# A gated recurrence and a causal-convolution unit: 1024-token chunks, the gated input on GpSimd, pairs of tokens transposed as 32-bit words

## Chip, cores, metric

One core of one Trainium2 chip (trn2). The metric is the device time in microseconds of one execution; medians are over all executions of a run, ratios over its fast ones.

## The reference, cut

Inputs `x`, `r_gate`, `i_gate` are (4, 6336, 256) in fp32: 25,344 tokens of 256 channels.

```python
log_a = 8.0 * sigmoid(r_gate) * log(clip(sigmoid(a_param), 1e-6, 1 - 1e-6))
a_t = exp(log_a)
x_gated = sqrt(max(1 - a_t * a_t, 1e-6)) * sigmoid(i_gate) * x
for t in range(S):                      # the scan, fresh in each of the 4 sequences
    h = a_t[:, t] * h + x_gated[:, t]
    y[:, t] = h
gate = sigmoid(causal_conv(y, conv_w))  # 5 taps per channel
out = (gate * (y @ w_val)) @ w_out
```

## The kernel before

Tokens arrive on the partitions; the scan wants channels there, so gates and products are transposed on TensorE. All sigmoids are tanh with a factor of a half: the input gate is (1 + tanh)/2. Windows are 512 tokens.

```python
# loads: 128 partitions x 4 runs of 1 KB (one token each)
nc.sync.dma_start(dst, src[t0:t0 + nj * P, :].rearrange("(j p) d -> p j d", p=P))
# tanh of both gates (ScalarE), u = (tanh + 1) * x in one VectorE instruction
nc.scalar.activation(out=tri[...], in_=ri[...], func=ACT.Tanh, scale=0.5)
nc.vector.scalar_tensor_tensor(out=uring[...], in0=tri[:, 1, ...], scalar=1.0, in1=xt[...], op0=ALU.add, op1=ALU.mult)
# a = exp(...) (ScalarE, from the transposed gate), a*a (GpSimd), sqrt in batches (ScalarE)
nc.gpsimd.tensor_tensor(out=ering[...], in0=a, in1=a, op=ALU.mult)
# xg = transpose(u) * norm, then the scan: both inputs in SBUF
nc.vector.tensor_tensor(out=xg[...], in0=uT[...], in1=nh[...], op=ALU.mult)
nc.vector.tensor_tensor_scan(out=yb[...], data0=aring[...], data1=xg[...], initial=..., op0=ALU.mult, op1=ALU.add)
# ... cut: conv as 5 diagonal 128x128 matmuls a half, val, gv = (tanh + 1) * val, out, copies, store
```

Of the kernel before, what the change touches and what calls it, by code (L numbers as in the profile page):

```python
# [8 lines left out]
P = 128  # L9
WIN = 512  # L10
SUB = WIN // P
CONV_K = 5
C_SCALE = 8.0
NS = 11
NY = 7
NIN = 3
NTRI = 3
NOSB = 3
MIN_UNIT = [1, 2, 3, 4]
COST = dict(load=4.5, tanh=1.9, u2=1.3, srT=0.5, uT=0.5, exp=1.45, e=2.15, xg=0.66, scan=2.7, conv=2.4, tg=0.97,  # L20
            val=0.95, gv=1.16, out=0.47, osbD=0.64, osbA=0.62, sq=0.88, sq0=0.2, table=1.3, store=1.5,
            sem=0.15, dma=2.2)
FP32 = mybir.dt.float32
# [5 lines left out]
def make_plan(frac):  # L29




    nw = len(frac)
    nq = [max(1, round(2 * f)) for f in frac]
    qwin = [(g, i) for g in range(nw) for i in range(nq[g])]
    qlast = [sum(nq[:g + 1]) - 1 for g in range(nw)]
    done, nxt, free = {}, {}, {}
    order, units = [], []
    mode = "E"  # L40

    def at(op):
        return nxt.get(op, 0)

    while True:
        cands = []

        def cand(op, eng, dur, deps, prio, i, n=1):
            t = 0.0
            for d in deps:  # L50
                if d[1] < 0:
                    continue
                if d not in done:
                    return
                t = max(t, done[d] + COST["sem"])
            if eng == "ACT" and op != "osb" and (op == "sq") != (mode == "S"):
                dur = dur + COST["table"]
            cands.append((max(free.get(eng, 0.0), t), prio, op, eng, dur, i, n))

        def per_window(op, eng, prio, deps, limit=nw):  # L60
            g = at(op)
            if g < limit:
                cand(op, eng, COST[op] * frac[g], [(d, g + o) for d, o in deps], prio, g)

        nsq = at("sq")
        per_window("load", "DMA", 0, [("tanh", -NIN), ("u2", -NIN)])
        per_window("tanh", "ACT", 3, [("load", 0), ("srT", -NTRI), ("u2", -NTRI)])
        per_window("u2", "DVE", 0, [("tanh", 0), ("uT", -NS)])
        per_window("srT", "PE", 0, [("tanh", 0), ("exp", -2)])
        per_window("exp", "ACT", 1, [("srT", 0), ("scan", -NS), ("e", -NS)])  # L70
        per_window("e", "POOL", 0, [("exp", 0), ("xg", -NS)])
        per_window("uT", "PE", 1, [("u2", 0), ("xg", -1)], nsq)
        per_window("xg", "DVE", 3, [("uT", 0), ("sq", 0), ("scan", -1)], nsq)
        per_window("scan", "DVE", 2, [("xg", 0), ("val", -NY)], nsq)
        per_window("conv", "PE", 3, [("scan", 0), ("tg", -1)])
        per_window("tg", "ACT", 0, [("conv", 0), ("gv", -2)])
        per_window("val", "PE", 2, [("conv", 0), ("gv", -1)])
        g = at("gv")
        if g < nw:
            cand("gv", "DVE", COST["gv"] * frac[g],  # L80
                 [("tg", g), ("val", g), ("out", qlast[g - 2] if g >= 2 else -1)], 1, g)
        q = at("out")
        if q < len(qwin):
            cand("out", "PE", COST["out"], [("gv", qwin[q][0]), ("osb", q - 1)], 1, q)
        q = at("osb")
        if q < len(qwin):
            for e, eng in (("D", "DVE"), ("A", "ACT")):
                cand("osb", eng, COST["osb" + e], [("out", q), ("store", qwin[q][0] - NOSB)], 0.5, q)
        g = at("store")
        if g < nw:  # L90
            cand("store", "DMA", COST["store"] * frac[g], [("osb", qlast[g])], -1, g)

        n = at("e") - nsq
        if n and mode == "E":
            all_in = at("exp") == nw
            stuck = at("e") == at("exp") and (all_in or ("scan", at("exp") - NS) not in done
                                              and at("exp") >= NS)
            low = (nsq - at("scan")) * (COST["xg"] + COST["scan"]) <= 2 * COST["table"] + COST["sq"] * n
            enough = n >= min(MIN_UNIT[min(len(units), len(MIN_UNIT) - 1)], nw - nsq)
            if stuck or (low and enough):  # L100
                cand("sq", "ACT", COST["sq0"] + COST["sq"] * sum(frac[nsq:nsq + n]),
                     [("e", nsq + n - 1)], -1, nsq, n)
        if not cands:
            break
        t, prio, op, eng, dur, i, n = min(cands)
        free[eng] = t + dur
        order.append((t, op, i, eng, n))
        nxt[op] = i + n
        for k in range(i, i + n):
            done[(op, k)] = t + dur + (COST["dma"] if eng == "DMA" else 0.0)  # L110
        if op == "sq":
            units.append(n)
        if eng == "ACT" and op != "osb":
            mode = "S" if op == "sq" else "E"
    assert at("store") == nw
    order.sort(key=lambda o: o[0])
    return order, qwin
# [3 lines left out]
def kernel(  # L121
# [15 lines left out]
    T = B * S  # L137

# [4 lines left out]

    nwin = (T + WIN - 1) // WIN
    ntok = [min(WIN, T - g * WIN) for g in range(nwin)]

    segs = []
    for g in range(nwin):
        t0, t1 = g * WIN, g * WIN + ntok[g]
        cuts = [t0] + [c for c in range(S, T, S) if t0 < c < t1] + [t1]  # L150
        segs.append([(c0 - t0, c1 - t0, c0 % S == 0) for c0, c1 in zip(cuts[:-1], cuts[1:])])
    YW = WIN + 4 * max(len(s) for s in segs)

    plan, qwin = make_plan([n / WIN for n in ntok])

    const = ctx.enter_context(tc.tile_pool(name="const", bufs=1))
    inp = ctx.enter_context(tc.tile_pool(name="inp", bufs=3))
    live = {}

    def load(g):  # L160
        nj = ntok[g] // P
        t0 = g * WIN
        ri = inp.tile([P, 2, SUB, D], FP32, name="ri", tag="ri", bufs=NIN)
        xt = inp.tile([P, SUB, D], FP32, name="xt", tag="xt", bufs=NIN)
        for dst, src in ((ri[:, 0, 0:nj, :], rf), (ri[:, 1, 0:nj, :], if_), (xt[:, 0:nj, :], xf)):
            nc.sync.dma_start(dst, src[t0:t0 + nj * P, :].rearrange("(j p) d -> p j d", p=P))
        live["ri", g], live["xt", g] = ri, xt

    with tc.manual_schedule():
        ap2 = const.tile([H, P], FP32, name="ap2")  # L170
        nc.sync.dma_start(ap2[:], a_param.rearrange("(h p) -> h p", p=P))
        wrow = const.tile([CONV_K, D], FP32, name="wrow")
        nc.sync.dma_start(wrow[:], moe_conv_w[:, :])
        for g in range(NIN):
            load(g)
# [7 lines left out]
        wv = const.tile([P, H, D], BF16, name="wv")  # L183
        nc.gpsimd.dma_start(wv[:], moe_w_val.rearrange("(hk p) n -> p hk n", p=P))
        wo = const.tile([P, H, D], BF16, name="wo")
        nc.gpsimd.dma_start(wo[:], moe_w_out.rearrange("(hk p) n -> p hk n", p=P))
        khf = const.tile([P, H], FP32, name="khf")
        wcol = const.tile([P, H, CONV_K], FP32, name="wcol")
        with tc.tile_pool(name="ps_setup", bufs=1, space=bass.MemoryType.PSUM) as ps_setup:
            kps = ps_setup.tile([P, H], FP32, name="kps")  # L190
            nc.tensor.transpose(out=kps[:], in_=ap2[0:H, :], identity=ident_f[0:H, 0:H])
            kt = const.tile([P, H], FP32, name="kt")
            nc.scalar.activation(out=kt[:], in_=kps[:], func=ACT.Tanh, scale=0.5)
            ksig = const.tile([P, H], FP32, name="ksig")
            nc.vector.tensor_scalar(out=ksig[:], in0=kt[:], scalar1=0.5, scalar2=0.5,
                                    op0=ALU.mult, op1=ALU.add)
            nc.vector.tensor_scalar(out=ksig[:], in0=ksig[:], scalar1=1e-6, scalar2=1.0 - 1e-6,
                                    op0=ALU.max, op1=ALU.min)
            kln = const.tile([P, H], FP32, name="kln")
            nc.scalar.activation(out=kln[:], in_=ksig[:], func=ACT.Ln)  # L200
            nc.vector.tensor_scalar(out=khf[:], in0=kln[:], scalar1=0.5 * C_SCALE, scalar2=None, op0=ALU.mult)
            wc_ps = ps_setup.tile([P, H, CONV_K], FP32, name="wc_ps")
            for h in range(H):
                nc.tensor.transpose(out=wc_ps[:, h, :], in_=wrow[0:CONV_K, h * P:(h + 1) * P],
                                    identity=ident_f[0:CONV_K, 0:CONV_K])
            nc.vector.tensor_copy(out=wcol[:], in_=wc_ps[:])
# [25 lines left out]
        def op_load(g, eng, n):  # L232
            if g >= NIN:
                load(g)
# [176 lines left out]
```

## Time and profile before

| | before |
|---|---|
| time, median | 374.97 us (374.37 to 377.16) |
| busy: VectorE / ScalarE / GpSimd | 334.6 / 312.4 / 138.3 us |
| granted TensorE clock | 0.942 |

Busy time is what an engine spends inside instructions, also where such an instruction is slowed by another engine.

### The profile page before, as it was taken

To read this page: it belongs to the slowest core of one execution; us is meant where nothing else is said; L and a number is where in the kernel's file an instruction comes from. 1 tells how busy PE (TensorE), PEld (TensorE's weight loads), DVE (VectorE), ACT (ScalarE), POOL (GpSimd) and SP (SyncE) were. 2 spreads that over 40 slices of the span, in tenths; PEclk is the share of its full clock that TensorE was granted. 3 is DMA by queue.
4 is the path that set the end of the run, shared out by engine and by line. 5 is a ranking of instruction groups with operands and counts; after the bars stand their busy time and mean duration, and the time that the engine had idled before them with its cause. 6 is when DMAs were issued, how large, how long until landed. Compare 5 with 4: busy or idle time off the path is not lost.

```text
span 372.5 us, 5299 instructions
## 1 busy us (share of the span) xinstructions
PE 272.4 (73%) x1933; PEld 159.9 (43%) x1933; DVE 334.6 (90%) x326; ACT 312.4 (84%) x298; POOL 138.3 (37%) x111
## 2 busy tenths in 40 slices
PE   0362779877686969877677887696976696869994
PEld 0232445444445535434344454363543363435543
DVE  3363999999999979999999999999999999999982
ACT  4898899999998799998967989789997997873342
POOL 2234435634362726434425324451655056300000
PEclk9995699999899899999889989789999899999998
DMA  8999996999999989996889979979999895313333
GB/s 210 355 348 353 356 350 201 298 353 339 345 361 324 330 268 361 352 364 202 280 264 339 351 226 295 356 255 344 301 323 336 278 340 187 127 56 114 113 114 141
DMA packets 105160, 104.42 MB, mean 280 GB/s; under 512 B 3240, under 2 KB 105135, under 8 KB 105135
## 3 DMA queue, kind: packets, MB, share of 16 engines
q1 hardware_dynamic: 104590, 103.83, 85.7%
q0 software_dynamic: 544, 0.26, 0.5%
q8 instruction: 15, 0.25, 0.3%
q14 instruction: 11, 0.08, 0.1%
HBM read 78.39 MB, written 25.95 MB: 280 GB/s over the span
## 4 chain that ended last, share of the span: by engine, by line
DVE 34%; ACT 23%; issue 19%; PE 14%; DMA 5%; POOL 2%; DVEq 0%; ACTq 0%
DVE yring L306 13%; DVE uring L246 8%; DVE gv L344 7%; ACT tri L240 6%; ACT ering L277 5%; PE gp L321 5%; PE ops L356 4%; ACT aring L257 4%; DMA xt<-in_x_dram 3%; DVE xg L290 3%; PE val L338 3%; ACT tg L327 3%; DVE osb L367 2%; ACT L327 2%; ACT L277 2%
## 5 line engine op out<-in xcount | busy, mean ns | idle before, releaser
L262 POOL TENSOR_TENSOR ering<-aring 128x1024 f32<-128x1024 f32 (+1 forms) x50 | 105.7, 2121 | 140.9 <-ACT aring L257 121.8
L321 PE MATMUL gp<-yring,diag 128*128 128x512 bf16 (+4 forms) x530 | 124.5, 384 | 24.7 <-DVE yring L306 14.2
L306 DVE TENSOR_TENSOR_SCAN yring<-aring,yring,xg 128x512 bf16<-128x512 f32 (+4 forms) x98 | 139.5, 1464 | 0.7
L240 ACT ACTIVATE tri<-ri 128x2048 bf16<-128x2048 f32 (+1 forms) x50 | 94.4, 1907 | 0.0
L321 PEld LDWEIGHTS <-diag 128*128 128x128 bf16 x530 | 50.8, 102 | 83.5 <-issue 16.3
L356 PE MATMUL ops<-wo,gv 128*128 128x256 bf16 x396 | 61.8, 280 | 26.2 <-DVE gv L344 12.4
L257 ACT ACTIVATE aring<-srT,khf 128x512 f32<-128x512 bf16 (+1 forms) x100 | 71.8, 791 | 3.4 <-PE srT L228 2.2
L246 DVE SCALAR_TENSOR_TENSOR uring<-tri,xt 128x1024 bf16<-128x1024 bf16 (+1 forms) x50 | 67.4, 1356 | 7.0 <-ACT tri L240 6.9
L327 ACT ACTIVATE tg<-gp 128x1024 bf16<-128x1024 f32 (+1 forms) x50 | 51.1, 1023 | 25.7 <-PE gp L321 21.2
L344 DVE SCALAR_TENSOR_TENSOR gv<-tg,val 128x1024 bf16<-128x1024 bf16 (+1 forms) x50 | 59.7, 1194 | 2.5 <-PE val L338 1.7
L304 POOL COPY yring<-yring 128x8 bf16<-128x8 bf16 x49 | 31.6, 644 | 77.4 <-DVE yring L306 77.4
L356 PEld LDWEIGHTS <-gv 128*128 128x128 bf16 x396 | 36.7, 99 | 50.0 <-DVE gv L344 20.2
L338 PE MATMUL val<-yring,wv 128*128 128x512 bf16 (+4 forms) x212 | 52.1, 371 | 5.3 <-DVE gv L344 5.3
L228 PE MATMUL srT<-ident_b,tri 128*128 128x128 bf16 x396 | 33.4, 232 | 22.2 <-ACT tri L240 22.2
L277 ACT ACTIVATE ering<-ering,b 128x3072 bf16<-128x3072 f32 (+2 forms) x21 | 47.0, 2280 | 0.1
L369 ACT COPY osb<-ops 128x512 f32<-128x512 f32 x46 | 27.2, 592 | 22.2 <-PE ops L356 19.1
L367 DVE COPY osb<-ops 128x512 f32<-128x512 f32 x53 | 36.1, 682 | 9.2 <-PE ops L356 8.0
L228 PE MATMUL uT<-ident_b,uring 128*128 128x128 bf16 x396 | 33.3, 232 | 15.0 <-DVE xg L290 14.7
L228 PEld LDWEIGHTS <-tri 128*128 128x128 bf16 x396 | 27.0, 104 | 33.2 <-ACT tri L240 27.1
L290 DVE TENSOR_TENSOR xg<-uT,ering 128x1024 bf16<-128x1024 bf16 (+1 forms) x50 | 33.7, 675 | 6.2 <-ACT ering L277 6.2
L228 PEld LDWEIGHTS <-uring 128*128 128x128 bf16 x396 | 28.3, 104 | 20.0 <-issue 14.3
L338 PEld LDWEIGHTS <-wv 128*128 128x128 bf16 x212 | 19.9, 99 | 18.9 <-issue 6.6
(31 smaller groups left out, 53.3 us busy)
## 6 DMA issues: line engine op xcount, KB each, us to landing
ri<-in_r_gate_dram SPq DMA_DIRECT2D x49, 512.0 KB, 6.1
ri<-in_i_gate_dram SPq DMA_DIRECT2D x49, 512.0 KB, 7.4
xt<-in_x_dram SPq DMA_DIRECT2D x49, 512.0 KB, 7.3
out_dram<-osb SPq DMA_DIRECT2D x49, 512.0 KB, 4.6
ri<-in_r_gate_dram SPq DMA_DIRECT2D x1, 256.0 KB, 7.0
ri<-in_i_gate_dram SPq DMA_DIRECT2D x1, 256.0 KB, 7.2
xt<-in_x_dram SPq DMA_DIRECT2D x1, 256.0 KB, 6.6
out_dram<-osb SPq DMA_DIRECT2D x1, 256.0 KB
```

Of the source, the lines that this page charges most:

```text
L228: nc.tensor.transpose(out=dst[:, h, j * P:(j + 1) * P], in_=src[:, j, h * P:(h + 1) * P], identity=ident_b[:])
L240: nc.scalar.activation(out=tri[:, :, 0:nj, :], in_=ri[:, :, 0:nj, :], func=ACT.Tanh, scale=0.5)
L246: nc.vector.scalar_tensor_tensor(out=uring[:, g % NS, 0:nj, :], in0=tri[:, 1, 0:nj, :], scalar=1.0, in1=xt[:, 0:nj, :], op0=ALU.add, op1=A ...
L257: nc.scalar.activation(out=aring[:, g % NS, h, 0:ntok[g]], in_=srT[:, h, 0:ntok[g]], func=ACT.Exp, scale=khf[:, h:h + 1], bias=khf[:, h:h ...
L262: nc.gpsimd.tensor_tensor(out=ering[:, g % NS, :, 0:ntok[g]], in0=a, in1=a, op=ALU.mult)
L277: nc.scalar.activation(out=nring[:, sl:sl + k, 0:H * WIN], in_=ering[:, sl:sl + k].rearrange("p s h t -> p s (h t)"), func=ACT.Sqrt, scale ...
L306: nc.vector.tensor_tensor_scan(out=yb[:, h, o:o + c1 - c0], data0=aring[:, g % NS, h, c0:c1], data1=xg[:, h, c0:c1], initial=0.0 if fresh ...
L321: nc.tensor.matmul(out=gp[:, h, c0:c1], lhsT=diag[:, h, kk, :], rhs=yb[:, h, o:o + c1 - c0], start=(kk == 0), stop=(kk == CONV_K - 1))
L327: nc.scalar.activation(out=tg[:, :, 0:ntok[g]], in_=live.pop(("gp", g))[:, :, 0:ntok[g]], func=ACT.Tanh, scale=0.5)
L338: nc.tensor.matmul(out=val[:, m, c0:c1], lhsT=wv[:, hk, m * P:(m + 1) * P], rhs=yb[:, hk, o:o + c1 - c0], start=(hk == 0), stop=(hk == H - 1))
L344: nc.vector.scalar_tensor_tensor(out=gv[:, :, 0:ntok[g]], in0=live.pop(("tg", g))[:, :, 0:ntok[g]], scalar=1.0, in1=live.pop(("val", g))[: ...
L356: nc.tensor.matmul(out=ops[:, e, :], lhsT=gv[:, hk, p0:p0 + P], rhs=wo2[:, hk, :], start=(hk == 0), stop=(hk == H - 1))
```

## The change

Its intent is to relieve VectorE: the product with x moves to GpSimd, the scan takes its second input from PSUM, instructions become twice as long, transfers move 4 KB runs, and two bf16 tokens are transposed as one 32-bit word. For that a pair of tokens must lie side by side; "two ways" says who puts them there. In the first (`WORDS` 1) both tanh write in steps of two elements and GpSimd reads x in steps; in the second (`WORDS` 2) only the r gate's tanh does, and VectorE's multiplication reads in steps. The fused (t + 1) * x has too many dimensions in the first way (by the author's account), so the change makes it two GpSimd instructions, an add of 1 in place and a product. The order of all operations is a fixed list.

```diff
+CHUNKS = [256, 512, 1024, ... 1024, 512, 256, 256]
+U_DVE = [0, 1, 2, 3]
+WORDS = [0, 0, 2, 2, 1, 1, 1, 1, 1, 1, 1, 1, 1, 1, 2, 2, 2, 2, 2, 2, 2, 2, 2, 2, 2, 1, 1, 1]
-        dst, src[t0:t0 + nj * P, :].rearrange("(j p) d -> p j d", p=P)
+        return dram[start[c] + o:start[c] + o + n, :].rearrange("(p q) d -> p q d", q=n // P)
+            for e in range(2):                                            # op_tanh
+                s = s.rearrange("p (w b d) -> p w b d", b=2, d=D)
+                if e == 0 or WORDS[c] == 1:
+                    o = o.rearrange("p (w d b) -> p w b d", b=2, d=D)     # written in steps
+                else:
+                    o = o.rearrange("p (w b d) -> p w b d", b=2, d=D)
+                nc.scalar.activation(out=o, in_=s, func=ACT.Tanh, scale=0.5)
+        def op_s1(k, bank):
+            t = tri[:, c % NRI, 1, 0:CHUNKS[c] * H]
+            nc.gpsimd.tensor_scalar(out=t, in0=t, scalar1=1.0, scalar2=0.0, op0=ALU.add, op1=ALU.add)
-            nc.vector.scalar_tensor_tensor(out=uring[:, g % NS, 0:nj, :], ...)   # u, all windows
+            if c in U_DVE:
+                nc.vector.scalar_tensor_tensor(out=u, in0=t, scalar=1.0, in1=xt, op0=ALU.add, op1=ALU.mult)
+            else:
+                nc.gpsimd.tensor_tensor(out=u, in0=t, in1=xt, op=ALU.mult)
-                        data1=xg[:, h, c0:c1],
+            nc.vector.tensor_tensor_scan(..., data0=aring[:, c % NA, h, 0:n], data1=src, ...)  # src in PSUM
+                    for r, h, col in QUADS:                               # op_conv: four 64x64 tiles a tap
+                        nc.tensor.matmul(out=pp[col * HP:(col + 1) * HP, b0 + d0:b0 + d1],
+                                         lhsT=diag[r * HP:(r + 1) * HP, h, kk, :], ...)
 ... cut: word transposes with an fp32 identity, the list of operations, setup
```

## The prediction

> **What bounds the kernel now.** I read, in this order: the page's busy times, the table of stretches, the groups by shape, the view of single lines, one timeline, and the DMA queues.
>
> ```profile
> PE 272.4 (73%) x1933; PEld 159.9 (43%) x1933; DVE 334.6 (90%) x326; ACT 312.4 (84%) x298; POOL 138.3 (37%) x111
> ```
>
> Two engines are close to full, VectorE and ScalarE; GpSimd has 234 us free. The stretches (columns: length, PE, PEld, DVE, ACT, POOL busy, clock, DMA share, GB/s) say where:
>
> ```profile
> 100.00:200.00 100.00, 77.99 (x568) 46.09 (x567) 96.25 (x90) 90.44 (x88) 41.65 (x31) 0.95 0.96 312
> 200.00:300.00 100.00, 75.03 (x535) 44.17 (x534) 97.57 (x88) 89.86 (x84) 43.14 (x31) 0.93 0.95 308
> 300.00:340.00 40.00, 31.29 (x230) 18.21 (x228) 38.73 (x38) 30.50 (x32) 12.73 (x13) 1.00 0.49 165
> ```
>
> In the body VectorE is 96 to 98% busy and the 16 DMA engines are 95% busy: two limits at once, with ScalarE at 90% behind them. After 300 us the loads are done and VectorE alone finishes. What fills it (by shape: busy us, mean ns):
>
> ```profile
> L306 DVE TENSOR_TENSOR_SCAN yring<-aring,yring,xg 128x512 bf16<-128x512 f32 x90 | 134.5, 1535 | 0.6
> L240 ACT ACTIVATE tri<-ri 128x2048 bf16<-128x2048 f32 x49 | 93.4, 1925 | 0.0
> L257 ACT ACTIVATE aring<-srT,khf 128x512 f32<-128x512 bf16 x98 | 70.7, 795 | 3.4 <-PE srT L228 2.2 <-issue 1.2
> L246 DVE SCALAR_TENSOR_TENSOR uring<-tri,xt 128x1024 bf16<-128x1024 bf16 x49 | 66.8, 1369 | 7.0 <-ACT tri L240 6.9
> L344 DVE SCALAR_TENSOR_TENSOR gv<-tg,val 128x1024 bf16<-128x1024 bf16 x49 | 59.0, 1204 | 2.5 <-PE val L338 1.7 <-ACT tg L327 0.8
> L367 DVE COPY osb<-ops 128x512 f32<-128x512 f32 x53 | 36.1, 682 | 9.2 <-PE ops L356 8.0
> ```
>
> The scan's mean hides two kinds. First the spread (min/median/max ns), then two moments of the timeline:
>
> ```profile
> L306 DVE TENSOR_TENSOR_SCAN yring<-aring,yring,xg x98: 319/1270/2985, 36.9 to 359.2; 128x512 bf16<-128x512 f32 x90, 128x192 bf16<-128x192 f32 x2, 128x384 bf16<-128x384 f32 x2, 128x64 bf16<-128x64 f32 x2
> ```
>
> ```profile
> 160.00 2.46 DVE L306 TENSOR_TENSOR_SCAN yring<-aring,yring,xg 128x512 bf16<-128x512 f32 x2
> ...
> 164.95 5.75 DVE L306 TENSOR_TENSOR_SCAN yring<-aring,yring,xg 128x512 bf16<-128x512 f32 x2
> 164.97 4.66 POOL L262 TENSOR_TENSOR ering<-aring 128x1024 f32<-128x1024 f32 x2 [2.15 <-ACT aring L257]
> ```
>
> Two scans take 2.46 us alone and 5.75 us beside GpSimd's squaring of a. Against 1.23 us each, the 90 scans lose about 90 x (1.535 - 1.23) = 27 us, and the u products 49 x (1.369 - 1.20) = 8 us.
>
> ```profile
> q1 hardware_dynamic: 104590, 103.83, 85.7%
> ```
>
> One packet takes 0.857 x 372.5 us x 16 / 104,590 = 49 ns for 1 KB.
>
> **What the Trainium skill says.** "SBUF — State Buffer", Who interferes with whom: a VectorE instruction with two SBUF inputs contends with a GpSimd instruction that reads SBUF. The trace agrees: 2.46 against 5.75 us. "DMA: Bandwidth & Descriptors", Specifications and Why small descriptors are slow: about 27 GiB/s per engine, a fixed cost per packet. It agrees in kind: 1 KB would be some 38 ns at 27 GB/s, and 49 are seen. "GPSIMD Engine Reference", Performance pitfalls: reads stepped by over 8 bytes cost about 2.9 instead of 1.9 cycles an element; no instruction here shows it. "TensorEngine Tiling (Array Packing)", Tiling Modes: 64x64 gives four independent tiles; nothing here shows that either.
>
> **The change, part by part.** 25,344 tokens make 28 chunks: 23 of 1024, five smaller; 51 pieces of up to 512.
>
> VectorE. *Scan*: data1 now comes from PSUM, so one SBUF input is left and the collisions go. From 64 columns (326 ns) to 512 alone (1213 ns) the slope is 1.98 ns, the fixed part 0.2 us: 50,688 x 1.98 ns + 56 x 0.2 = 112 us, was 139.5. *u*: only the first four chunks stay, 5,632 elements, 6.4 us, was 67.4; the other 24 chunks go to GpSimd. *xg*: 680 ns now for 1024 bf16. In 13 chunks (26 pieces) the operands are read in steps; I take the one-element rate, gv's 1.2 us: 31 us, and 16 for the rest: 47, was 33.7. *gv*: 59.7, unchanged. *Output copy*: 40 of 51 pieces, of twice the old width: 682 + 512 x 1.04 = 1.22 us, 47.5 us, was 36.1. Setup 3.5. Sum **276 us**, 58 less.
>
> ScalarE. Tanh: as many elements in 52 instructions, 95 us, if a stepped fp32 read costs nothing (no row shows it). Exp: 100 instructions of 512 become 56, 46 of them of 1024; 71.8 us / 100 = 0.72 each, plus 0.427 for 512 more elements = 1.15: 53 + 6 for small ones = 58.5, was 71.8. Sqrt 48 (47.0 now), tg 51 (51.1). Output copies: 11, about 10.5 us, was 27.2. Table loads: 11 sqrt batches give 22, plus 3 at the start, 25 x 1.283 = 32. Sum **295 us**, 17 less. ScalarE thus becomes the longest engine.
>
> GpSimd. Squares: 50,688 elements at 1.89 us per 1024 (the median now) = 94 us. Products: 45,056 elements at the same rate = 83, plus 19 for stepped reads of x in half of them (estimate: one more cycle, from the page above). One-input adds of 1: taken as half the two-input cost, 42. The small boundary copies (31.6 us) go. Sum **238 us**, was 138, within the span.
>
> DMA. 25,350 packets of 4 KB; estimate 4096/27.2 + 11 = 162 ns each, over 16 engines: 257 us, was 319. That limit goes away.
>
> TensorE. Per 512 tokens now: conv 2.33, val 1.03, out 1.2, transposes 1.22: 5.8 us. Then: conv as five rounds of four tiles 1.17, val 1.03, out 1.2, and 12 word transposes instead of 16. At today's 76 ns each that is 0.9, together 4.3 us, 213 us in all.
>
> **The path that sets the end.** Everything overlaps, so sums of engines do not add. ScalarE starts when the first 256-token gates land, about 6 us (7.6 now with twice the bytes). Up to its last square root (sixteen us of tg and copies come later) it has 295 - 16 = 279 us of work. I allow it 97% busy, what VectorE reaches now as the bound: 288 us. After that comes a drain, in which VectorE by the given order still has 27 us of work (the last scans of chunks 23 to 27, their products, gates and a few copies), then the last copy and store, 3 us. 6 + 288 + 30 = **324 us**. As a check, VectorE: 276 / 0.97 + 13 before its first scan (18.4 now) + 3 at the end = 300, so it is the second limit, 24 us below.
>
> **Rivals.** (1) *The word transposes are slow.* They carry fp32, and no row shows such a 128x128 one. At four times 76 ns TensorE needs 7.0 us per 512 tokens, 349 us in all: 365 to 385, no gain. For it: stepped PSUM outputs; against it: somebody chose to replace fewer bf16 ones with them. (2) *GpSimd becomes the bound.* If adds run at the two-input rate and stepped reads cost twice the guess, 94 + 83 + 38 + 83 = 298 us, in a chain ahead of every scan: 330 to 345. For it: it was idle and gets all new work; the change varies which engine reads in steps, as if GpSimd were short. (3) *Stepped tanh reads cost on ScalarE.* At half rate in three quarters of tanh's work: +70 us, 380 or more. (4) *Collisions were worth more than I count*, and the fixed order fits well: VectorE and ScalarE both near 98% and a drain half as long: 300 to 308. For it: VectorE's 96% in the body was full of waits inside scans, and the order names banks, so it was fitted.
>
> **Range and chances.** The mean of my path is 324; (4) pulls to 302, (2) to 345. (1) and (3) have some 3% each. Range 302 to 348. Faster by over 2% (below 367.4): 0.94; within 2%: 0.04; slower: 0.02.
>
> **What would show each step right or wrong.** Scans of 1024 at 2.2 to 2.4 us whether GpSimd works or not; ScalarE the busiest at 285 to 300 us with VectorE at 270 to 285; GpSimd 225 to 260; packets of 4 KB and a DMA share of 0.7 to 0.85 in the body; tanh at 1.9 us per 2048 in both layouts; word transposes near 80 ns. Tanh over 2.5 us, transposes over 200 ns apiece or GpSimd over 290 us would break it.

One slip to know while reading it: the tanh steps lie in its bf16 output (4 bytes apart), not in its fp32 input as the text says.

## The result and the profile after

The changed kernel takes 410.58 us (407.38 to 412.33), right result. The ratio is 1.093 (95% interval 1.087 to 1.099): 9% slower. All ratios here are the mean time of one kernel's fast runs over that of the other's of the same rounds, so not quite the ratio of the medians quoted. Executions over 1.5% slower than the fastest of the same kernel are left out of the means.

Page of the kernel after, busy times:

```profile
PE 269.7 (66%) x2379; PEld 181.2 (44%) x2411; DVE 272.6 (67%) x225; ACT 306.9 (75%) x215; POOL 342.8 (84%) x116
```

VectorE lost 62 us of work, as intended. GpSimd went from 138 to 343 us and is now the longest engine. The stretches (columns as before):

```profile
60.00:100.00 40.00, 26.10 (x216) 18.47 (x218) 23.55 (x18) 36.56 (x22) 39.80 (x13) 0.82 0.72 275
100.00:200.00 100.00, 61.74 (x517) 41.79 (x523) 59.13 (x46) 70.30 (x44) 99.87 (x28) 0.81 0.68 250
200.00:300.00 100.00, 74.13 (x694) 49.20 (x704) 78.84 (x57) 76.98 (x50) 99.69 (x32) 0.88 0.72 269
300.00:340.00 40.00, 29.96 (x253) 20.31 (x257) 29.39 (x21) 28.42 (x20) 40.00 (x11) 0.79 0.78 302
```

From 60 to 340 us GpSimd has less than 1 us of idle time in 280; every other engine has slack. The groups by shape (busy us, mean ns):

```profile
L350 POOL TENSOR_SCALAR ri<-ri 128x2048 bf16<-128x2048 bf16 x21 | 148.6, 7087 | 2.1 <-ACT ri L308 2.1
L441 DVE TENSOR_TENSOR_SCAN yring<-aring,yring,pp 128x1024 bf16<-128x1024 f32 x46 | 106.9, 2338 | 5.0 <-PE pp L428 4.8
L308 ACT ACTIVATE ri<-ri 128x2048 bf16<-128x2048 f32 x46 | 104.1, 2333 | 25.3 <-DMA ri<-in_r_gate_dram 25.3
L365 POOL TENSOR_TENSOR uring<-ri,xr 128x2048 bf16<-128x2048 bf16 x21 | 88.9, 4237 | 0.3
L342 POOL TENSOR_TENSOR ering<-aring 128x1024 f32<-128x1024 f32 x46 | 86.2, 1896 | 14.3 <-ACT aring L336 14.3
...
L498 DVE COPY osb<-pp 128x1024 f32<-128x1024 f32 x38 | 46.2, 1215 | 14.6 <-PE pp L488 12.8 <-issue 1.6 <-ACT tg L464 0.2
```

The first line is the surprise: the add of 1 takes 7.09 us for 2048 bf16 elements, longer than the product of two tensors (4.24) beside it. With its small forms it is 156 us. It is no wait for another engine: by the view of its line the median is 7.085 and the longest 7.097 us. The view of the scan's line shows that the collisions are gone (min/median/max):

```profile
L441 DVE TENSOR_TENSOR_SCAN yring<-aring,yring,pp x54: 722/2339/2348, 28.4 to 399.8; 128x1024 bf16<-128x1024 f32 x46, 128x512 bf16<-128x512 f32 x4, 128x256 bf16<-128x256 f32 x4
```

Median and maximum differ by 9 ns, where before the median was 1270 and the maximum 2985. GpSimd's timeline in the body has no gaps:

```profile
161.17 5.61 POOL L342 TENSOR_TENSOR ering<-aring 128x1024 f32<-128x1024 f32 x3
166.73 14.15 POOL L350 TENSOR_SCALAR ri<-ri 128x2048 bf16<-128x2048 bf16 x2
180.85 8.73 POOL L365 TENSOR_TENSOR uring<-ri,xr 128x2048 bf16<-128x2048 bf16 x2
189.53 1.91 POOL L342 TENSOR_TENSOR ering<-aring 128x1024 f32<-128x1024 f32 x1
```

And the waits, first of the DMA queue, then of ScalarE (us in total, times, longest):

```profile
SPq L221 <- POOL uring L365: 181.4, 21, 17.0
```

```profile
ACT ering L374 <- POOL ering L342: 35.5, 6, 10.4
ACT ri L308 <- DMA ri<-in_r_gate_dram: 25.3, 5, 10.0
```

These are one thing seen three times. The loads wait 181 us for GpSimd to finish products and so free the gate buffers; ScalarE then waits for those late loads, and for squares that stand behind adds in GpSimd's queue. The lines with DMA and ScalarE in them are not causes. So is the clock: 0.855 against 0.942, and 0.930 again in the first experiment below.

The span adds up from GpSimd alone: 30 us idle before 60 us, 343 us of work, and 34 us from its last product (end at 373.8) to the end: 407 of 407.7.

### The profile page after: what moved, and what is told of

Same layout as the page of the kernel before. It is cut to its first block, busy times and chain, and to the rows that moved or that the text cites. A ratio compares the mean times of both kernels' runs of the same rounds, so it can differ in the third digit from the quotient of the medians.

```text
span 407.7 us, 6095 instructions
## 1 busy us (share of the span) xinstructions
PE 269.7 (66%) x2379; PEld 181.2 (44%) x2411; DVE 272.6 (67%) x225; ACT 306.9 (75%) x215; POOL 342.8 (84%) x116
## 4 chain that ended last, share of the span: by engine, by line
POOL 26%; DMA 20%; PE 19%; issue 16%; ACT 10%; DVE 4%; SPq 3%; DVEq 0%; POOLq 0%; ACTq 0%
POOL uring L365 11%; DMA xr<-in_x_dram 10%; POOL ri L350 9%; DMA ri<-in_r_gate_dram 8%; POOL ering L342 6%; PE pp L453 6%; ACT ri L308 4%; PE pp L488 3%; PE pp L472 3%; ACT ering L374 3%; PE pp L395 2%; SPq L221 2%; DVE yring L441 2%; PE pp L428 2%; PE pp L324 2%
## 5 line engine op out<-in xcount | busy, mean ns | idle before, releaser
L350 POOL TENSOR_SCALAR ri<-ri 128x2048 bf16<-128x2048 bf16 (+2 forms) x24 | 156.1, 6513 | 2.1 <-ACT ri L308 2.1
L308 ACT ACTIVATE ri<-ri 128x2048 bf16<-128x2048 f32 (+2 forms) x52 | 109.5, 2175 | 25.3 <-DMA ri<-in_r_gate_dram 25.3
L441 DVE TENSOR_TENSOR_SCAN yring<-aring,yring,pp 128x1024 bf16<-128x1024 f32 (+2 forms) x54 | 114.5, 2139 | 5.7 <-PE pp L428 4.8
L342 POOL TENSOR_TENSOR ering<-aring 128x1024 f32<-128x1024 f32 (+2 forms) x56 | 94.0, 1698 | 27.7 <-ACT aring L336 27.7
L365 POOL TENSOR_TENSOR uring<-ri,xr 128x2048 bf16<-128x2048 bf16 (+2 forms) x24 | 93.6, 3906 | 0.3
L453 PE MATMUL pp<-yring,diag 64*64 64x512 bf16 (+15 forms) x1196 | 77.1, 384 | 18.4 <-ACT tg L464 10.4
L478 DVE SCALAR_TENSOR_TENSOR gv<-tg,pp 128x1024 bf16<-128x1024 bf16 (+1 forms) x51 | 60.2, 1180 | 40.9 <-ACT tg L464 32.5
L336 ACT ACTIVATE aring<-pp,khf 128x1024 f32<-128x1024 bf16 (+2 forms) x56 | 60.7, 1119 | 8.0 <-PE pp L324 7.3
L464 ACT ACTIVATE tg<-pp 128x1024 bf16<-128x1024 f32 (+1 forms) x51 | 50.7, 994 | 19.9 <-PE pp L453 17.2
L488 PE MATMUL pp<-wo,gv 128*128 128x256 bf16 x396 | 54.4, 282 | 7.3 <-DVE gv L478 6.9
```

The source lines that it names most:

```text
L308: nc.scalar.activation(out=o, in_=s, func=ACT.Tanh, scale=0.5)
L336: nc.scalar.activation(out=dst, in_=src, func=ACT.Exp, scale=khf[:, h:h + 1], bias=khf[:, h:h + 1])
L342: nc.gpsimd.tensor_tensor(out=ering[:, c % NE, h * n:(h + 1) * n], in0=a, in1=a, op=ALU.mult)
L350: nc.gpsimd.tensor_scalar(out=t, in0=t, scalar1=1.0, scalar2=0.0, op0=ALU.add, op1=ALU.add)
L365: nc.gpsimd.tensor_tensor(out=u, in0=t, in1=xt, op=ALU.mult)
L441: nc.vector.tensor_tensor_scan(out=yring[:, h, y0:y0 + n], data0=aring[:, c % NA, h, 0:n], data1=src, initial=prev, op0=ALU.mult, op1=ALU.add)
```

## The experiments

Theory A: the add is the whole cause, and the rest of the change behaves as predicted. Rival B: the rest is slow too (word transposes, stepped tanh, late loads), and a relieved GpSimd uncovers it.

| run | GpSimd busy, us | time, us | ratio to before (95%) |
|---|---|---|---|
| after | 342.8 | 410.6 | 1.093 (1.087 to 1.099) |
| one_op | 305.1 | 376.3 | 1.002 (0.996 to 1.008) |
| plus1_tt | 276.3 | 350.5 | 0.932 (0.926 to 0.937) |
| ts_fp32 (wrong result) | 248.5 | 341.5, one run | |
| copy_pool (wrong result) | 229.2 | 343.0, one run | |
| no_plus1 (wrong result) | 188.1 | 342.3 | 0.910 (0.903 to 0.917) |

**no_plus1.** The add left out. Its output is wrong, which doesn't matter for the time.

```diff
-            nc.gpsimd.tensor_scalar(out=t, in0=t, scalar1=1.0, scalar2=0.0, op0=ALU.add, op1=ALU.add)
+            return
```

> The add of 1 on GpSimd is left out and nothing else; the result is wrong on purpose. Theory A (the add is the whole cause: 156 us of GpSimd's 343 us): GpSimd falls to about 187 us, ScalarE becomes the longest engine again at about 305 us, and the time falls to 320 to 340 us, near the 324 predicted. Rival B (the rest is slow too: fp32 transposes at some 230 ns each, stepped tanh at 2.48 us, the loads late): it stays above 355 us, with TensorE or ScalarE waits in place of the GpSimd ones.

Measured 342.27 us (339.94 to 343.91). Stretches of the body:

```profile
100.00:200.00 100.00, 83.23 (x781) 54.86 (x781) 86.22 (x67) 99.15 (x63) 67.32 (x27) 0.95 0.91 344
200.00:300.00 100.00, 84.49 (x832) 57.21 (x833) 96.75 (x68) 92.08 (x66) 68.38 (x30) 0.97 0.86 316
```

ScalarE (99%, then 92%) and VectorE (86%, then 97%) are full and GpSimd is not. Removing 155 us of GpSimd work took 68 us off the time and put it well below the kernel before, inside the predicted range though 18 us above the predicted value. Theory A stands for the slowdown; B falls, but for those 18 us, taken up below.

**one_op.** The second operation, which added 0, taken away.

```diff
-... tensor_scalar(out=t, in0=t, scalar1=1.0, scalar2=0.0, op0=ALU.add, op1=ALU.add)
+... tensor_scalar(out=t, in0=t, scalar1=1.0, scalar2=None, op0=ALU.add)
```

> The same add as one arithmetic operation instead of two (the second one added 0). If the instruction pays per arithmetic operation, 7.09 us per 2048 elements fall to about 3.6 us, GpSimd to 265 us, and the time to about 340 us. If it pays per element whatever the operations, it stays at 7 us and 410 us.

Measured 376.25 us (374.47 to 378.16); group by shape:

```profile
L350 POOL TENSOR_SCALAR ri<-ri 128x2048 bf16<-128x2048 bf16 x21 | 112.6, 5374 | 2.1 <-ACT ri L308 2.1
```

Neither expectation held: the second operation costs 1.71 us of 7.09. It is useless work worth 34 us of the time, as GpSimd's 38 us less came off nearly whole.

**plus1_tt.** The add as a sum with a broadcast tile of ones, on GpSimd.

```diff
+        ones = const.tile([P, D], BF16, name="ones")
+        nc.vector.memset(ones[:], 1.0)
-            nc.gpsimd.tensor_scalar(out=t, ...)
+            t = t.rearrange("p (k n) -> p k n", n=D)
+            nc.gpsimd.tensor_tensor(out=t, in0=t, in1=ones[:].unsqueeze(1).to_broadcast([P, CHUNKS[c] * H // D, D]), op=ALU.add)
```

> The add on GpSimd as a sum of two tensors, the second a broadcast tile of ones. If the two-input rate of the squares and products (about 2 ns an element) holds, 4.1 us in place of 7.09 for 2048 elements, GpSimd about 275 us, time 340 to 355 us: two inputs would then be faster than one. If the cost lies in bf16 out or in the update in place, it stays near 7 us and 410 us.

Measured 350.46 us (347.49 to 351.06), right result:

```profile
L353 POOL TENSOR_TENSOR ri<-ri,ones 128x2048 bf16<-128x2048 bf16 x21 | 85.3, 4075 | 2.1 <-ACT ri L310 2.1
```

A second tensor input is cheaper than a constant, 4.08 against 5.37 us: as expected by the theory, with bf16 and in place, so neither of these is the cause. GpSimd is still 99.6% busy from 60 to 300 us (239.0 of 240).

**copy_pool.** A copy in place (wrong on purpose; one run, state unknown).

```diff
-            nc.gpsimd.tensor_scalar(out=t, ...)
+            nc.gpsimd.tensor_copy(out=t, in_=t)
```

> A plain copy in place on GpSimd at the place of the add (wrong result on purpose): no arithmetic. One operation took 5.37 and two 7.09 us per 2048 elements, so 1.72 us an operation; if that line holds, the copy takes about 3.65 us, GpSimd about 265 us, and the time is 343 to 352 us. If the copy takes 5 us or more, the line is wrong and the first operation is nearly free.

```profile
L350 POOL COPY ri<-ri 128x2048 bf16<-128x2048 bf16 x21 | 39.6, 1893 | 13.7 <-ACT ri L308 13.7
```

1.89 us, not 3.65: the straight line through one and two operations was wrong. The first operation with a constant is the dear one, 3.5 us more than a copy; the second adds 1.7. With 24 of these copies 42 us, this is just the cost that the prediction gave to the adds, and the time, 343.0 us, is that of no add at all: GpSimd at 229 us is hidden. It lies in the expected 343 to 352 us although the duration expected was wrong.

**ts_fp32.** One operation over the same bytes as 1024 fp32 words (0 added; one run, state unknown).

```diff
-            nc.gpsimd.tensor_scalar(out=t, ...)
+            t = t.bitcast(FP32)
+            nc.gpsimd.tensor_scalar(out=t, in0=t, scalar1=0.0, scalar2=None, op0=ALU.add)
```

> On GpSimd one arithmetic operation with a constant over the same bytes taken as 1024 fp32 words instead of 2048 bf16 (0 is added, so the bits stay; wrong result on purpose). If the cost is per element whatever the type, half of 5.37 us, 2.6 to 2.8. If bf16 is what makes it slow (a conversion each way), clearly less, 1 to 2 us.

```profile
L351 POOL TENSOR_SCALAR ri<-ri 128x1024 f32<-128x1024 f32 x21 | 58.1, 2774 | 7.8 <-ACT ri L308 7.8
```

2.71 ns an element, against 2.62 in bf16, as the first expectation said: the cost is per element and, of these two types, neither is clearly cheaper. What inside this instruction makes it slower than a two-tensor sum stays open.

**plus1_dve.** The add on VectorE.

```diff
-            nc.gpsimd.tensor_scalar(out=t, ...)
+            nc.vector.tensor_scalar(out=t, in0=t, scalar1=1.0, scalar2=None, op0=ALU.add)
```

> The add on VectorE instead of GpSimd, at the same place in the order. Theory A: VectorE takes 24 x about 0.7 us more, 17 us, and has room (273 us before); the time is 325 to 345 us, right result. Rival B: above 355 us. If VectorE has to wait for GpSimd at each of these adds, they show as 2 to 5 us each and the time lies above that of the kernel without the add by 20 us or more.

Measured 351.46 us (350.96 to 353.14), right result, ratio 0.937 (0.932 to 0.941); the view of its line:

```profile
L350 DVE TENSOR_SCALAR ri<-ri x24: 260/683/3233, 41.3 to 308.3; 128x2048 bf16<-128x2048 bf16 x21, 128x512 bf16<-128x512 bf16 x2, 128x1024 bf16<-128x1024 bf16 x1
```

0.68 us mostly, a tenth of GpSimd's 7.09, and up to 3.23. The timelines of both engines show why. The six adds that start while a GpSimd instruction runs end 0.28 to 0.56 us after that instruction does (one runs from 64.67 to 67.90 us, beside a product from 62.97 to 67.34); the other 18 take 0.26 to 0.69 us. So an add waits for the GpSimd instruction that it meets. The time is 9 us above no_plus1 and 6 above the expected range: VectorE, 97% busy from 200 to 300 us, has no room for 22 us more.

**tanh_flat.** As no_plus1, and tanh writes straight. Its output is wrong, which doesn't matter for the time. This tests the open 18 us.

```diff
-                if e == 0 or WORDS[c] == 1:
+                if False:
```

> As the kernel without the add, and every tanh writes its output straight instead of in steps of two elements (wrong result on purpose, same work otherwise). 33 of the 2048-element tanh instructions take 2.50 us stepped and 1.92 straight: ScalarE does 19 us less, some 286 us. If ScalarE's work sets the end once GpSimd is out of the way, 342 becomes 322 to 328 us, the predicted 324. If VectorE (97% busy in the last 100 us of the body) takes over at once, it stays at 336 to 342 us.

Measured 326.60 and 329.71 us in two fast executions, mean 328.2; the two others, 331.63 and 331.66, are slow, at clocks no lower. First two views of the tanh line in no_plus1 (all instructions, min/median/max; then the long ones), then of this run, then its busy times:

```profile
L308 ACT ACTIVATE ri<-ri x52: 763/2496/2612, 16.6 to 296.1; 128x2048 bf16<-128x2048 f32 x46, 128x512 bf16<-128x512 f32 x4, 128x1024 bf16<-128x1024 f32 x2
L308 ACT ACTIVATE ri<-ri 128x2048 bf16<-128x2048 f32 x46 | 104.5, 2350 | 0.2 <-DMA ri<-in_r_gate_dram 0.2
```

```profile
L308 ACT ACTIVATE ri<-ri 128x2048 bf16<-128x2048 f32 x46 | 85.4, 1913 | 0.1
```

```profile
PE 253.9 (77%) x2411; PEld 171.7 (52%) x2411; DVE 269.1 (82%) x225; ACT 286.3 (87%) x215; POOL 188.0 (57%) x92
```

ScalarE loses 19 us and the time 14 (fast mean 342.1 to 328.2). So the stepped writes account for about three quarters of the 18 us. The fast executions lie at the upper edge of the first expectation and past it; that VectorE holds the rest, as the second had it, is not shown.

**conv128.** plus1_tt with the convolution in 128x128 matmuls again.

```diff
-                    for r, h, col in QUADS:
+                    for h in range(H):
-                                         lhsT=diag[r * HP:(r + 1) * HP, h, kk, :], ...
+                                         lhsT=diag[:, h, kk, :], ...
-HALVES = ((0, 128), (192, 64))
+HALVES = ((0, 64), (128, 192))
... cut: diag as 128x128 matrices, out without the quarters
```

> The two-input add, and the convolution back in 128x128 matmuls (two per tap instead of four 64x64 ones). From 1.27 us for a piece of 512 tokens to about 2.35: TensorE does 51 x 1.08 = 55 us more, to some 310 us. If TensorE's latency is in the path (tg waits for the convolution), 360 us or more; if it hides, 350 us as in the variant with the two-input add.

Measured 360.96 us (359.86 to 362.64), ratio 0.959 (0.952 to 0.966) against plus1_tt's 0.932. ScalarE's waits, first in plus1_tt, then here:

```profile
ACT tg L467 <- PE pp L456: 14.7, 18, 1.6
```

```profile
ACT tg L467 <- PE pp L456: 32.5, 24, 3.1
```

As the first expectation said: the small tiles are worth about 10 us, and ScalarE's waits for the convolution are 18 us shorter with them.

**xfer_1k.** plus1_tt with 1 KB transfers (tokens in another order, wrong).

```diff
-.rearrange("(p q) d -> p q d", q=n // P)
+.rearrange("(q p) d -> p q d", q=n // P)
```

> The variant with the two-input add, and every transfer as before in 1 KB runs (tokens land in another order, so the result is wrong on purpose; all instructions and sizes are the same). At the 49 ns of the kernel before, 101,000 packets take 310 us of 16 engines, against 279 us now; the loads of the body, at a DMA share of 0.85 to 0.89 so far, would need more than the engines have. If transfers are in the path: 358 to 375 us. If they hide: 350 us.

Measured 353.29 us (352.25 to 353.70), ratio 0.940 (0.936 to 0.945). The queue of plus1_tt, then of this run (packets, MB, share of 16 engines):

```profile
q1 hardware_dynamic: 29968, 104.35, 81.1%
```

```profile
q1 hardware_dynamic: 105232, 104.35, 91.1%
```

81.1% of 345.6 us are 280 us, 91.1% of 351.5 are 320 us: 4 KB runs save 40 us of DMA work. Of that 3 us or 1% reach the time, and this is hardly resolved. Mostly it hides: the second expectation (350 us) fits, the first (358 to 375) does not.

**tt_w2.** plus1_tt with the second layout for all chunks from the third on.

```diff
-WORDS = [0, 0, 2, 2, 1, 1, ... 1]
+WORDS = [0, 0] + [2] * 26
```

> The two-input add, and every chunk from the third on in the second layout (product contiguous, multiplication on VectorE in steps). ScalarE: 13 stepped tanh fewer at 0.58 us for the 1024-token ones, about 6 us less; GpSimd: about 0.3 us less in each of 10 chunks, 3 us; VectorE: 20 multiplications at 1.21 instead of 0.68 us, 11 us more. With GpSimd as the bound at 276 us: 343 to 350 us. If VectorE is in the path: 352 to 358 us.

Measured 347.39 us (345.35 to 347.95), ratio 0.923 (0.916 to 0.930), right result. As expected; the two ways trade 6 us of ScalarE (306.0 to 299.9) and 3 of GpSimd (276.3 to 273.3) for 10 of VectorE (271.6 to 281.3), and its interval overlaps that of plus1_tt.

**u_dve_w2.** The product back on VectorE with the add fused, second layout.

```diff
-U_DVE = [0, 1, 2, 3]
+U_DVE = list(range(len(CHUNKS)))
-            nc.gpsimd.tensor_scalar(out=t, ...)
+            return
```

> The gated product back on VectorE, add fused, as in the kernel before; the rest as changed, all chunks in the second layout (the first one has too many dimensions for that instruction). VectorE: 272 + 20 x 0.53 + 24 products of up to 2048 at about 2.27 us alone, 50 us, makes 335 us, plus collisions with GpSimd's squares. Time 360 to 375 us. If the move to GpSimd was what mattered, this is 10 us or more above the variant with the two-input add; if not, it is the same.

Measured 394.00 us (390.57 to 396.19), ratio 1.045 (1.036 to 1.054), above the expected 360 to 375:

```profile
PE 276.6 (71%) x2411; PEld 179.6 (46%) x2411; DVE 332.6 (85%) x249; ACT 300.7 (77%) x215; POOL 105.1 (27%) x68
```

VectorE's 332.6 us are as reckoned, but it reaches only 85% of the span, with ScalarE waiting 45 us for TensorE's convolutions and 30 us for its transposes. The fixed order was made for products on GpSimd, and how much of the 47 us above tt_w2 is the order and how much the move stays open. That moving the product off VectorE helps, given a cheap add, is shown for this order only.

**mixed** and **mixed_w2e.** The add shared: on VectorE for some chunks, the two-input sum on GpSimd for the others.

```diff
+            if WORDS[c] == 1:        # mixed;  mixed_w2e: if c < 12, and the second layout throughout
+                nc.vector.tensor_scalar(out=t, in0=t, scalar1=1.0, scalar2=None, op0=ALU.add)
+                return
+            ... the sum with ones, as in plus1_tt
```

> The add of 1 on VectorE for the 13 chunks whose product reads x in steps (4 to 13 and the last three), and as a two-input sum on GpSimd for the other 11. If both earlier variants were held by one full engine each (GpSimd 99% busy in the one, VectorE 97% in the other), sharing gives 340 to 346 us, at the 342 us of the kernel without the add, with ScalarE's 306 us as the bound. If ScalarE's order held both already, it stays at 350 us.

> A try at the best version, right result: second layout for all chunks, the add on VectorE for chunks 4 to 11 and as a two-input sum on GpSimd afterwards. GpSimd about 243 us, ScalarE 300, VectorE about 288. If ScalarE's path sets the end, 338 to 345 us; below that only if GpSimd's full stretch in the first half held the 347 us of the variant with the second layout.

mixed: 347.48 us (343.18 to 349.03, of which the last is slow; fast mean 346.0, between the two expectations), ratio 0.919 (0.909 to 0.929). mixed_w2e: 349.58 us (347.53 to 350.39), ratio 0.929 (0.924 to 0.935), a miss. Both right. Neither is clearly better than tt_w2: with GpSimd at 233 to 276 us the right versions lie between 347 and 351 us. mixed and tt_w2 are the fastest right kernels, about 8% below the kernel before and 15% below the changed one.

## Why the prediction was wrong

The mechanism was half right, and one term decided. A slower result had been given a chance of 0.02; the prediction's own sign of being wrong, "GpSimd over 290 us", is what came, with 343. By its own steps:

| step | predicted, us | measured, us |
|---|---|---|
| VectorE sum (kernel after) | 276 | 272.6 |
| of it scans | 112 | 114.5 |
| of it stepped and straight products with the norm | 47 | 46.5 |
| ScalarE sum | 295 | 306.9 |
| of it tanh | 95 | 112.5 |
| GpSimd squares | 94 | 94.0 |
| GpSimd products, stepped reads counted | 83 + 19 | 93.6 |
| **GpSimd adds of 1** | **42** | **156.1** |
| DMA work | 257 | 279 |
| TensorE sum | 213 | 269.7 (no_plus1: 258.7) |

1. **The term that failed** is "One-input adds of 1: taken as half the two-input cost, 42." No row of the kernel before showed such an instruction; the figure was an analogy, that one input must cost less to read than two. The runs show 3.46 ns an element for the add as written and 2.62 with one operation, against 1.99 for two tensors and 0.92 for a copy. The analogy fits the copy exactly and the add not at all. 114 us too little there, and 8 too much in the products, made the GpSimd sum 238 instead of 343 us.

2. **The step after it**, "within the span", compared a sum of busy time with a span. GpSimd starts late (30 us idle) and 34 us of work follow its last product; its limit was its sum plus 64 us. With 238 that is 302, still hidden below 324; with 343 it is 407.

3. **Rival (2) named the right engine and was sized wrong twice**: adds at the two-input rate were its worst case, and to its own 298 us it did not add that head and drain, which gives 362, not 330 to 345. A rival that rests on the only unmeasured rates in the sum deserved more than the part it got in the range.

4. **The contention step was right**: 1024-token scans at 2.34 us whatever GpSimd does, and VectorE's sum right within 4 us.

5. **The path with ScalarE as the bound** fits as soon as the add is out of the way, but with two terms too small. It is shown for ScalarE in the first half of the body (99% busy); in the second VectorE is the fuller one (97 against 92%). In no_plus1 the last square roots end at 311.5 us:

```profile
309.08 2.37 ACT L374 ACTIVATE ering<-ering,b 128x1024 bf16<-128x1024 f32 x3
```

The drain from there to 341.7 is 30.2 us; 30 was predicted. That is partly luck: VectorE has 22.0 us of work in it, not 27, and more idle time. Ahead of it 311.5 stands in place of 294. ScalarE does 289.6 us of work up to there, not 279, and idles 22 us where 15 were allowed (6 at the start and 3% of 288). tanh_flat shows 14 us of this to be the stepped writes (2.50 us against 1.92 for 2048 elements, by the prediction "if a stepped fp32 read costs nothing").

6. **Rival (1)**, slow word transposes, did not come true. Two lines of TensorE's timeline in the kernel before, then two in no_plus1:

```profile
153.79 0.61 PE L228 MATMUL srT<-ident_b,tri 128*128 128x128 bf16 x8
...
163.12 2.33 PE L321 MATMUL gp<-yring,diag 128*128 128x512 bf16 x10 [1.63 <-ACT tg L327]
```

```profile
199.88 0.66 PE L324 MATMUL pp<-ident_f,ri 128*128 128x128 f32 x4
...
212.15 1.27 PE L453 MATMUL pp<-yring,diag 64*64 64x512 bf16 x20
```

Four word transposes take 0.66 us, where eight bf16 ones took 0.61: dearer each by 2.2, not by four. The main path had taken them at 76 ns each, and they took 165: 576 of them make 51 us more, about what its TensorE sum lacks. TensorE had the room. The convolution of a 512-token piece takes 1.27 us, against 2.33; 1.17 was predicted. Rival (3), stepped tanh, came true in kind, 0.58 us an instruction, at a quarter of its feared size (17.5 of 70 us). Rival (4), 300 to 308 us, came true in no run.

7. **DMA** was right in kind (a slip on the way: it took 27 GiB/s for 27 GB/s, so its 38 ns for 1 KB should be 35): 0.684 x 407.7 = 279 us against 319 before, and nearly all of the saving hidden (xfer_1k), as "That limit goes away" said.

## What to carry to other kernels

Work moved to an engine must be priced with a measured duration of that very instruction on that very engine; where none exists, the guess is the widest term of the sum and the range has to follow it. An engine that looks idle has, as its limit, its work plus the time before its first input and after its last output, not the whole span. And when an engine turns up full, read what its longest instruction is before replanning: here a second operation that adds zero cost 34 us, and the same sum written with two tensors took 60 us off.

## What the Trainium skill lacked or had wrong

- "GPSIMD Engine Reference", Engine selection, says of GpSimd that 1-input work is "roughly line-rate" and 2-input work about twice slower than VectorE. The second is so here: 4.12 us for a product of 2048, 2.28 for VectorE's fused one in no_plus1. The copy bears out the first (0.92 ns an element), an operation with a constant does not: 2.62 ns with one, 3.46 with two operations, slower than two tensors (1.99), and 8 to 10 times VectorE's 0.33 (0.683 us per 2048). A row for such instructions is missing. The same page's Performance pitfalls for Q7 kernels gives reads stepped by more than 8 bytes about 50% more time. In these products, with one of two inputs stepped by 1 KB between pairs, it was 4.40 against 4.12 us, 7%.
- "ScalarE: Activation LUTs" gives one rate per element for all functions and types. Nothing there tells that a bf16 output written 4 bytes apart is slower: 2.50 against 1.92 us for 2048 elements.
- No page gives the duration of a 128x128 transpose of fp32 words in a stream: four in 0.66 us here.
